# Output projection of a fused attention and gated feed-forward kernel: 32-row heads against dense rows of O

## The chip, the cores and the metric

The kernel runs on one core of a Trainium2 chip. A core has five engines with an instruction queue each: PE (TensorE, the matmul array, whose weight loads are listed as PEld), DVE (VectorE), ACT (ScalarE), POOL (GpSimd) and SP (SyncE, which here only issues transfers). They share the on-chip memory SBUF; PE writes its results into PSUM, eight banks of 128 partitions by 2 KB. Engines wait for one another through semaphores, and each carries out its queue in order. The metric is the device time of one execution in microseconds (us), as the median of several.

## The reference

```python
def _A_ref(x, wqkv, wo):                       # B, S, D = 1, 2048, 640
    H = 32; Dh = D // H                        # 32 heads of 20
    qkv = (x @ wqkv).reshape(B, S, 3, H, Dh).transpose(2, 0, 3, 1, 4)
    q, k, v = qkv[0], qkv[1], qkv[2]
    scores = jnp.einsum("bhqd,bhkd->bhqk", q, k) * Dh ** -0.5
    o = jnp.einsum("bhqk,bhkd->bhqd", softmax(scores), v)
    return o.transpose(0, 2, 1, 3).reshape(B, S, D) @ wo

def _B_ref(x, w1, b1, w2):                     # F = 1536
    h = x @ w1 + b1
    return (h * jnp.tanh(softplus(h))) @ w2

g = sigmoid((x * gate_w).sum(-1, keepdims=True))
return g * _A_ref(...) + (1 - g) * _B_ref(...)
```

Everything is bfloat16. The softmax of 32 heads over 2048 by 2048 scores is 134 million exponentials, which is most of the kernel.

## The kernel before

**Tiling.** Heads go in 8 groups `g` of four, queries in 4 chunks `c` of 512, keys in 16 tiles of 128. A unit is one head by one key tile by one chunk: a score matmul of 32 rows by 128 keys by 512 queries into one PSUM bank, its exponential, and a matmul with V (PV) of 21 columns, whose first column of ones gives the softmax's sum. There are 2048 units. Four heads lie on 32 partitions each, so score matmuls of different heads run side by side, and so do the four PV matmuls of a key tile, which accumulate in bank 6 (`ACC`).

**Two ways to an exponential.** A step (`emit_s`, `emit_e`) computes the scores of two or three units and exponentiates them with one ACT instruction over two or three banks (L1295, "128x1024" or "128x1536") into the ring `ETS`. Beside it DVE takes whole tiles of four units (`x_block`, `emit_x`): it turns each score bank into a 16-bit integer that is the bit pattern of an approximate exponential (L1353), makes two more copies with another offset (L1383), and PE multiplies all three with V, twice with V scaled by POOL (L1409). A tile on DVE so costs four L1353, two L1383, two L1409 and three sets of PV matmuls in place of one. Its bank is one of 7, 5 and 2 (`FLEX`), which `x_block` takes only if DVE or ACT has read it by the time that PE gets there. `third` decides by the same rule whether a step takes three banks.

**Between the steps** PE does tasks: the projections of q, k and v, the feed-forward's two products (`h_task`, `b_task`) and the output projection. They are cut into single accumulation steps, which fill what a step leaves of PE's time.

**After a group** (`group_done`): DVE copies ACC to `OUNG` (L1610), a transfer reads the sums into `RR` (L1613), DVE inverts them (L1617), two transfers spread them over partitions through DRAM (L1618, L1620, into `BCT`), and POOL multiplies (`times`, L1575). The result goes into `QT[:, g, chunk c]`, where the group's queries were: four heads, each on 32 partitions of which 21 carry something. For the program, SP's queue holds these transfers, the feed-forward's weights (L947), the moves of q and k through DRAM and the stores, all in one order.

**Output projection.** `p_task` makes one tile of 128 tokens by 320 columns: eight accumulation steps, one for each group, each with the 128 partitions of `QT` as weights in four quarters of 32 tokens (`quarters`, L526) and the 320 columns of a padded `wo` (`WOG`) streaming by. 24 such tiles belong to chunks 0 to 2. The last chunk's eight tiles are done in two parts, six groups ahead (`part_task`) and two at the very end (`p_task` with `rest`, or `late_mm`), as the last group's softmax ends only then. `load_wo` brings the padded weights and zeros between them.

**Order.** All of it is laid out ahead of time by a planner in the kernel's own Python (`Plan.add`): each operation has an estimated cost, each engine an estimated clock, and rules with some thirty constants decide what comes next. `STRETCHES` gives some of these constants other values from a step on. So any edit moves instructions everywhere.

Of the kernel before, what the change touches and what calls it, by code (L numbers as in the profile page):

```python
# [85 lines left out]
CROWD = 1.357  # L86
# [59 lines left out]

STRETCHES = {
    13: {"CALLED": 3.681, "CROWD": 1.516, "KEPT": 14, "LATER": 0.181, "NEED": 4, "OVER": 0.547, "ROOM": 1.615, "STREAM": 0.46},
    32: {"CALLED": 3.681, "CROWD": 0.992, "FMIN": 0.345, "KEPT": 8, "LATER": 0.181, "LOAD": 0.613, "NEED": 4, "OVER": 0.547, "PATIENCE": 2.71, "ROOM": 1.318, "SLACK": 0.305, "SPUN": 0.635, "STREAM": 0.413, "THIRD": 0.599, "XSLACK": 0.603},
    52: {"CALM": 5, "EAGER": 131, "LATER": 0.553, "OVER": 0.328, "VMIN": 1.54},  # L150
    74: {"BEHIND": 25.336, "CALM": 10, "FREE": 0.172, "MARGIN": -0.397, "ROOM": 1.73, "STREAM": 0.359, "THIRD": 0.926},
    96: {"BEHIND": 25.336, "CALM": 10, "EAGER": 156, "FMIN": 0.177, "FREE": 0.172, "LATER": 0.693, "MARGIN": -0.397, "ROOM": 1.73, "STREAM": 0.359, "THIRD": 0.926},
    118: {"AHEAD": 23, "BEHIND": 23.531, "BUSY": 0.465, "LOAD": 0.723, "NEED": 2, "PATIENCE": 11.956, "SPUN": 0.486, "THIRD": 1.082, "XSLACK": 0.459},
    140: {},
    159: {"BUSY": 0.52, "LATER": 0.268, "PATIENCE": 6.491, "SPUN": 0.578, "STREAM": 0.36},
    177: {"BUSY": 0.716, "FMIN": 0.404, "LATER": 0.268, "PATIENCE": 6.491, "SPUN": 0.578, "STREAM": 0.36},
    197: {"MARGIN": 0.991, "ROOM": 1.736, "XSLACK": 0.222},
    216: {"BEHIND": 24.715, "CALLED": 0.877, "LATER": 0.69, "MARGIN": 0.991, "ROOM": 1.736, "SLACK": 0.232, "SPUN": 0.618, "XSLACK": 0.222},
    236: {"AHEAD": 29, "BEHIND": 24.715, "BUSY": 1.142, "CALLED": 1.095, "KEPT": 12, "LATER": 0.493, "MARGIN": 0.991, "PATIENCE": 9.167, "ROOM": 1.736, "SLACK": 0.232, "SPUN": 0.643, "STREAM": 0.441, "VMIN": 0.744, "XSLACK": 0.222},
    257: {"AHEAD": 45, "BEHIND": 18.952, "BUSY": 1.117, "CALLED": 1.095, "FMIN": 0.076, "FREE": 0.133, "KEPT": 12, "LATER": 0.493, "MARGIN": 0.991, "OVER": 0.11, "PATIENCE": 9.167, "ROOM": 1.736, "SLACK": 0.321, "SPARED": 1, "SPUN": 0.643, "STREAM": 0.441, "VMIN": 0.744, "XSLACK": 0.222},  # L160
    276: {"BUSY": 0.321, "CALM": 4, "CROWD": 1.465, "EAGER": 157, "LOAD": 0.543, "MARGIN": 0.584, "NEED": 4, "PATIENCE": 11.808, "SLACK": 0.257, "SPARED": 1},
    298: {"FREE": 0.157, "LOAD": 0.615, "NEED": 4, "OVER": 0.168, "STREAM": 0.569, "VMIN": 1.094, "XLATE": 11.627},
    319: {"CROWD": 0.991, "FMIN": 0.126, "FREE": 0.036, "MARGIN": 1.148, "SPUN": 0.7},
    341: {"AHEAD": 44, "CROWD": 0.991, "EAGER": 115, "FMIN": 0.126, "FREE": 0.036, "MARGIN": -0.419, "SPUN": 0.668, "THIRD": 0.337},
    360: {"AHEAD": 44, "CROWD": 0.991, "EAGER": 115, "FMIN": 0.126, "FREE": 0.036, "MARGIN": -0.419, "NEED": 4, "SPUN": 0.668, "THIRD": 0.337, "XSLACK": 0.204},
    379: {"AHEAD": 44, "CALM": 5, "CROWD": 1.926, "EAGER": 90, "FMIN": 0.191, "FREE": 0.036, "MARGIN": -0.5, "NEED": 4, "PATIENCE": 12.367, "ROOM": 3.226, "SPARED": 1, "SPUN": 0.668, "THIRD": 0.447, "VMIN": 0.861, "XSLACK": 0.258},
    396: {"CROWD": 1.489, "SLACK": 0.54, "THIRD": 0.417, "XSLACK": 0.47},
    416: {"CROWD": 0.97, "EAGER": 44, "KEPT": 15, "LATER": 0.299, "OVER": 0.128, "STREAM": 0.521},
    438: {"CROWD": 0.97, "EAGER": 44, "FREE": 0.231, "KEPT": 15, "LATER": 0.299, "MARGIN": 0.28, "OVER": 0.128, "PATIENCE": 12.737, "STREAM": 0.521, "THIRD": 0.979, "VMIN": 0.916, "XLATE": 6.721},
    460: {"CROWD": 0.97, "EAGER": 44, "FREE": 0.231, "KEPT": 15, "LATER": 0.299, "MARGIN": 0.28, "OVER": 0.128, "PATIENCE": 12.737, "STREAM": 0.521, "THIRD": 0.979, "VMIN": 0.916, "XLATE": 6.721},  # L170
    481: {"CROWD": 0.97, "EAGER": 44, "FREE": 0.118, "KEPT": 15, "LATER": 0.299, "MARGIN": 0.28, "OVER": 0.06, "PATIENCE": 12.737, "SLACK": 0.161, "STREAM": 0.521, "THIRD": 1.171, "VMIN": 0.916, "XLATE": 6.721},
    501: {"CALLED": 0.845, "CALM": 4, "FMIN": 0.095, "LATER": 0.538, "ROOM": 3.669},
# [129 lines left out]
def bass_gated_mix__softmax_full_mha__dense_activation_mish__prompt_kernel(  # L302
# [123 lines left out]
    def attention(pl, fast):  # L426
# [1140 lines left out]
        def group_done(c, g, step, last):  # L1567
# [39 lines left out]
            while oung_free[m] == "busy":  # L1607
                (norm or lasting).popleft()[1]()
# [459 lines left out]
```

## Time and profile before

| what | value |
|---|---|
| median of 3 runs | 751.69 us (751.41 to 752.72) |
| the profiled execution | 750.51 us, of which the span from first to last instruction is 748.7 us |
| POOL busy | 358.0 us (48%), 695 instructions |
| PEld busy | 276.0 us (37%) |
| DMA | 50.49 MB, 67 GB/s on average, HBM read 39.01 MB and written 8.90 MB |
| granted PE clock | 0.998 of full speed |

The page's busy times are unions of intervals: an instruction counts from its start to its end, also where the next one has begun already. An engine that is 97% busy may thus still be slower than it could be. The idle time of an engine and what ended it stand beside each group of instructions.

### The profile page before, as it was taken

The page shows a single profiled execution, that of the slowest core. Times are in us where ns is not written, and L with a number is a line of the kernel's source. Part 1 is how long each engine was busy: PE and PEld are TensorE (multiplying, and loading weights), DVE is VectorE, ACT ScalarE, POOL GpSimd, SP SyncE. Part 2 cuts the span into 40 slices and gives each one's busy share as a digit, 9 for nine tenths or more (in the row PEclk, how much of TensorE's full clock was granted, in tenths as well). Part 3 has the DMA queues.
Part 4 walks back from the last instruction along what each step waited for, and adds up shares of the span by engine and source line. Part 5 has one row for each costly group of instructions (what it writes and reads, how often), then busy time and mean ns, then how long its engine had stood idle before and what let it go on. Part 6 is the DMA issues. An engine that isn't in the chain of part 4 may idle for free.

```text
span 748.7 us, 26101 instructions
## 1 busy us (share of the span) xinstructions
PE 724.3 (97%) x11336; PEld 276.0 (37%) x11336; DVE 681.1 (91%) x1173; ACT 730.1 (98%) x755; POOL 358.0 (48%) x695
## 2 busy tenths in 40 slices
PE   8999999999999999999999999999999999999996
PEld 3333334334433332233333433334343343333343
DVE  3799999889898989989999999999999999999985
ACT  6999999999999999999999999999999999999995
POOL 3304332115563547322458675163568758575331
PEclk9999999999999999999999999999999999999999
DMA  9312323123133422632132210112221221101001
GB/s 193 104 30 68 96 66 90 35 83 95 37 92 89 127 70 72 183 80 49 46 104 63 58 36 21 52 39 59 62 76 49 67 63 49 56 18 35 17 25 44
DMA packets 78020, 50.49 MB, mean 67 GB/s; under 512 B 21408, under 2 KB 73880, under 8 KB 77848
## 3 DMA queue, kind: packets, MB, share of 16 engines
q1 hardware_dynamic: 75528, 48.24, 23.4%
q8 instruction: 92, 1.51, 0.9%
q10 hardware_dynamic: 2256, 0.47, 0.3%
q14 instruction: 32, 0.26, 0.1%
q0 software_dynamic: 112, 0.01, 0.1%
HBM read 39.01 MB, written 8.90 MB: 64 GB/s over the span
## 4 chain that ended last, share of the span: by engine, by line
ACT 43%; PE 38%; DVE 14%; POOL 3%; issue 1%; DMA 0%; ACTq 0%; POOLq 0%
ACT ETS L1295 42%; PE PS L1268 13%; PE PS L1513 11%; PE PS L526 11%; DVE LN L1353 4%; DVE LN L1383 2%; POOL HB L1049 2%; DVE U L1048 1%; POOL U L1047 1%; DVE U L1052 1%; PE PS L847 1%; DVE HB L1009 1%; ACT W2R L1033 1%; DVE REG L1383 1%; DVE REG L1353 1%
## 5 line engine op out<-in xcount | busy, mean ns | idle before, releaser
L1295 ACT ACTIVATE ETS<-PS 128x1024 bf16<-128x1024 f32 (+1 forms) x724 | 708.5, 1134 | 5.3 <-PE PS L1268 3.6
L1268 PE MATMUL PS<-QT,KT 32*128 32x512 bf16 (+1 forms) x2130 | 285.9, 377 | 10.8 <-ACT ETS L1295 8.3
L1353 DVE TENSOR_SCALAR LN<-PS 128x512 int16<-128x512 f32 x412 | 274.7, 680 | 20.5 <-PE PS L1268 18.7
L1409 POOL TENSOR_SCALAR VS<-V_all 128x84 bf16<-128x84 bf16 x268 | 146.2, 546 | 93.5 <-PE PS L1513 51.3
L1268 PEld LDWEIGHTS PS<-QT,KT 32*128 32x128 bf16 x2130 | 72.3, 91 | 230.9 <-ACT ETS L1295 192.2
L1513 PE MATMUL PS<-ETS,V_all 128*21 128x512 bf16 (+1 forms) x1584 | 148.6, 375 | 0.2 <-ACT ETS L1295 0.2
L1383 DVE TENSOR_SCALAR LN<-LN 128x2048 int16<-128x2048 int16 x186 | 132.7, 717 | 5.6 <-PE PS L1513 4.9
L1049 POOL TENSOR_TENSOR HB<-U,HB 128x128 bf16<-128x128 f16 x192 | 93.1, 517 | 83.8 <-DVE U L1048 83.8
L1575 POOL TENSOR_TENSOR QT<-OUNG,BCT 128x128 bf16<-128x128 f32 x124 | 64.0, 546 | 119.2 <-DMA BCT<-SUMS 119.2
L526 PE MATMUL PS<-XB,REG 128*32 128x256 bf16 (+1 forms) x1800 | 88.0, 295 | 2.5 <-DVE LN L1353 1.0
L1513 PE MATMUL PS<-LN,VS 128*21 128x512 f16 (+1 forms) x844 | 79.0, 377 | 1.2 <-POOL VS L1409 1.0
L526 PE MATMUL PS<-W2R,HB 128*32 128x320 bf16 x1536 | 75.8, 301 | 0.6 <-issue 0.3
L1513 PEld LDWEIGHTS PS<-ETS,V_all 128*21 128x21 bf16 x1584 | 38.2, 90 | 54.5 <-issue 46.5
L1047 POOL TENSOR_SCALAR U<-REG 128x256 f16<-128x256 f32 x72 | 37.3, 541 | 36.3 <-ACT REG L1033 35.1
L526 PEld LDWEIGHTS PS<-XB,REG 128*32 128x32 bf16 x1800 | 42.2, 95 | 28.3 <-issue 19.1
L526 PE MATMUL PS<-WOQ,QT 128*32 128x320 bf16 x1024 | 50.7, 301 | 0.5 <-DVE QT L1601 0.3
L526 PEld LDWEIGHTS PS<-W2R,HB 128*32 128x32 bf16 x1536 | 35.1, 96 | 25.4 <-issue 13.7
L1513 PE MATMUL PS<-LN,V_all 128*21 128x512 f16 (+1 forms) x424 | 40.3, 376 | 0.0
L1353 DVE TENSOR_SCALAR REG<-PS 128x512 int16<-128x512 f32 x56 | 37.4, 679 | 2.9 <-PE PS L1268 2.8
L526 PE MATMUL PS<-XB,WOQ 128*32 128x512 bf16 (+2 forms) x440 | 35.6, 381 | 0.1
L1513 PEld LDWEIGHTS PS<-LN,VS 128*21 128x21 bf16 x844 | 19.9, 89 | 39.0 <-issue 17.9
L1048 DVE TENSOR_TENSOR U<-U 128x1024 f16<-128x1024 f16 x48 | 32.7, 681 | 0.2
(116 smaller groups left out, 531.9 us busy)
## 6 DMA issues: line engine op xcount, KB each, us to landing
REG<-in_B_w_dram SPq DMA_DIRECT2D x36, 320.0 KB, 3.3
BCT<-SUMS SPq DMA_DIRECT2D x31, 256.0 KB
W2R<-in_B_w_dram SPq DMA_DIRECT2D x12, 320.0 KB, 4.5
QT<-QS SPq DMA_DIRECT2D x28, 128.0 KB, 3.0
KT<-KS SPq DMA_DIRECT2D x28, 128.0 KB
KS<-LN SPq DMA_DIRECT2D x16, 128.0 KB, 4.3
QS<-WOQ SPq DMA_DIRECT2D x16, 120.0 KB
W2R<-in_B_w_dram SPq DMA_DIRECT2D x12, 160.0 KB, 4.3
```

What stands on the lines that cost most here:

```text
L526: last = e.matmul(to[at + j:at + j + n, :], w[:, j:j + n], x, start=start, stop=stop, tile_position=(0, at + j))
L847: return lambda e, bank: e.matmul(PS[:, bank, t * n:(t + 1) * n], xt(c)[:, f, t * P:(t + 1) * P], WV[:, f, g * HD:g * HD + n], start=(f == ...
L1047: lift = lambda e, at: e.tensor_scalar(A[:, at], U[:, at], LIFT, LIFT, ALU.mult, ALU.add)
L1048: times = lambda e, at: e.tensor_tensor(A[:, at], A[:, at], B[:, at], ALU.mult)
L1049: last = lambda e, at: e.tensor_tensor(h[:, at], A[:, at], h[:, at], ALU.mult)
L1268: op = pl.add("pe", lambda e, to=to, g=real(g), tile=tile, j=j, cols=cols, c=c, of_q=of_q: e.matmul(to[:, cols], KT[32 * j:32 * j + 32, g, ...
L1295: e_op[s] = pl.add("act", lambda e: e.activation(RING[:, p:p + n, :], scores(s)[:, 0:n, :], AF.Exp, scale=SCALE), [s_op[s], *(pv_slot[b] f ...
L1353: bank_free[bank] = x_ops[bank] = tile["op"] = dve(lambda e: e.tensor_scalar(dst, PS[:, bank, :], SCALE * ULPS, BASE, ALU.mult, ALU.add), ...
L1383: op = pl.add("dve", lambda e: e.tensor_scalar(to, src, SHADES[n] - SHADES[held], None, ALU.add), [made, *deps], cost=SHADE, lock=SHADE - ...
L1409: ops = [pl.add("pool", lambda e, i=i, n=n, src=src: e.tensor_scalar(VS[:, n, i, :, :], src, WEIGHTS[i + 1], None, ALU.mult), [v_done[(rea ...
L1513: lasts[n] = pl.add("pe", lambda e, v=v, j=j, src=src[:, cols], of_q=of_q, begin=begin, end=end: e.matmul(PS[32 * j:32 * j + EW, ACC, of_q ...
L1575: oung_free[m] = bc_read[0] = otn_done[(c, g)] = pl.add("pool", lambda e, some=some: e.tensor_tensor(otn(c, g)[:, some], src[:, some], BC[ ...
```

## The change

**Dense rows.** In the taken program, `times` is followed by transfers for 30 of the 31 groups that it serves (all but group 6 of the last chunk): `ship` writes the group's 128 by 512 to a DRAM scratch `OT`, `land` reads rows 1 to 16 of each of its four heads back to 64 dense partitions, two groups to one block of 128, and once for each chunk a further transfer brings the four rows that are left of all heads (17 to 20) as a fifth block. `ship` goes into the queue two steps after `times` (`SHIP`), `land` four steps after `ship` (`LAND`). `p_task` then has five accumulation steps instead of eight, `part_task` four instead of six; the last two groups of the last chunk stay as they were. `wo` is loaded in the new order of rows, with the padded form for the last two groups only.

**Banks.** `x_block` may take a bank that comes free up to `EARLY` later than PE gets there (0.35 us, in some stretches 0.17 to 0.55), and `third` one up to `SOON` later (0, in some stretches up to 0.28).

**Planning.** Two assumed lock times between DVE and POOL are changed, and all stretches have new constants, with new step numbers.

```diff
+EARLY = 0.35
+SOON = 0.0
+SHIP = 2
+LAND = 4
 STRETCHES = {
-    140: {},
+    141: {"BEHIND": 24.559, "CALLED": 1.144, "EARLY": 0.264, "KEPT": 12, "OVER": 0.186, "SPUN": 0.579},
...
+    OT = nc.dram_tensor("OT", [NC, H, 32, CW], BF16, kind="Internal")
...
+                wo_h = A_wo.rearrange("(h r) c -> h r c", r=DH)
+                pieces = [(f"wm{k}", WQ[:, k, :], wo_h[8 * k:8 * k + 8, 0:16, :], 0.9) for k in range(NFT - 1)]
+                pieces.append(("wr", WQ[:, NFT - 1, :], wo_h[:, 16:DH, :], 0.9))
+                pieces += [(f"wo{j}", WOP[32 * j + 1:32 * j + 1 + DH, :, :], wo_v[j, :, NG - 2:, :], 0.5) for j in range(HG)]
...
         def p_mm(c, t, half, g, groups):
+
+            if fast and g < NFT:
+                rows = P if c < NC - 1 or g < NFT - 1 else 16 * (NG - 2)
+                o, w = otn(c, g)[0:rows, t * P:(t + 1) * P], WQ[0:rows, g, half * HALF:(half + 1) * HALF]
+            else:
+                o, w = otn(c, g)[:, t * P:(t + 1) * P], (WOP[:, g - NG + 2, :] if fast else WOG[:, g, :])[:, half * HALF:(half + 1) * HALF]
...
+        if fast:
+            every = tuple(range(NFT))
+            early, late = (0, 1, 2, 4), (NG - 2, NG - 1)
...
-            if not x and late < THIRD or free is not None and free.t1 + HOP > begin:
+            if not x and late < THIRD or free is not None and free.t1 + HOP > begin + SOON:
...
-                return free is None or free.t1 + HOP <= begin
+                return free is None or free.t1 + HOP <= begin + EARLY
...
+                if fast and (c < NC - 1 or g < NG - 2):
+                    shipping.append((now["step"] + SHIP, lambda: ship(done)))
+                else:
+                    otn_done[(c, g)] = done
+
+            def ship(done):
+                slot = f"os{c % 2}{g % 2}"
+                shipped[(c, g)] = op = shipped[slot] = pl.add("sp", lambda e: e.dma_start(
+                    OT.ap()[c, HG * g:HG * g + HG, :, :].rearrange("j r t -> (j r) t"), otn(c, g)), [done, shipped.get(slot)],
+                    slot, cost=0.45, tail=2.5, bulk=0.3)
+                shipping.append((now["step"] + LAND, lambda: land(op)))
+
+            def land(op):
+                main = 64 * (g % 2)
+                last = g == (NG - 1 if c < NC - 1 else NG - 3)
+                slot = f"ot{c % 2}{g % 2}"
+                landed.setdefault(c, []).append(op)
+                done = otn_done[(c, g)] = landings[slot] = pl.add("sp", lambda e: e.dma_start(
+                    otn(c, g // 2)[main:main + 64, :], OT.ap()[c, HG * g:HG * g + HG, 1:17, :]), [op, landings.get(slot)],
+                    slot, cost=0.45, tail=2.5, bulk=0.2)
+                if last:
+                    rest_done[c] = pl.add("sp", lambda e: e.dma_start(
+                        otn(c, NFT - 1)[0:HD // 5 * (g + 1), :], OT.ap()[c, 0:HG * (g + 1), 17:21, :]), landed[c], f"or{c}",
+                        cost=0.45, tail=2.7, bulk=0.3)
```

Line numbers grow by 6 to 60 through the insertions: L1295 becomes L1321, L1268 L1294, L1513 L1539, L526 L532, L1353 L1379, L1383 L1409, L1613 L1668. Counted over the two programs, in the branch that is taken:

| engine, instruction | before | after |
|---|---|---|
| ACT, exponential of two banks / of three / of one | 642 / 81 / 1 | 700 / 36 / 0 |
| DVE, L1353 (a score bank to integers) | 520 | 540 |
| DVE, L1383 (a shifted copy) | 260 | 270 |
| POOL, L1409 (V scaled) | 268 | 278 |
| PE, quarters of the output projection (L526) | 1024 | 672 |
| PE, PV matmuls | 3192 | 3232 |
| PE, score matmuls | 2130 | 2126 |
| PE, fillers on the keys (L1806) | 8 | 4 |
| SP, transfers | 305 | 374 |

Three places in the two programs' order. The first is ACT, from the point where the kernel reads its safety flag (about a fifth into the program); `ETS` is the ring of exponentials, `W2R<-HB` the feed-forward's tanh. Before:

```order
L1295 ACTIVATE ETS<-PS 128x1024 x7
L1033 ACTIVATE W2R<-HB 128x1024
L1295 ACTIVATE ETS<-PS 128x1024 x2
L1295 ACTIVATE ETS<-PS 128x1536
L1295 ACTIVATE ETS<-PS 128x1024
L1295 ACTIVATE ETS<-PS 128x1536
L1295 ACTIVATE ETS<-PS 128x1024
L1295 ACTIVATE ETS<-PS 128x1536
L1295 ACTIVATE ETS<-PS 128x1024
L1295 ACTIVATE ETS<-PS 128x1536
L1033 ACTIVATE W2R<-HB 128x1024
```

and after:

```order
L1321 ACTIVATE ETS<-PS 128x1024 x3
L1321 ACTIVATE ETS<-PS 128x1536
L1321 ACTIVATE ETS<-PS 128x1024 x7
L1043 ACTIVATE W2R<-HB 128x1024
L1321 ACTIVATE ETS<-PS 128x1024 x11
L1043 ACTIVATE W2R<-HB 128x1024
L1321 ACTIVATE ETS<-PS 128x1024 x29
L1043 ACTIVATE W2R<-HB 128x1024
L1321 ACTIVATE ETS<-PS 128x1024 x32
```

The steps of three banks give way to steps of two, beside each of which DVE takes a bank.

The second is PE at the first tiles of the output projection, a little past the middle of the program; `WOQ,QT` are its quarters, four to an accumulation step. Before:

```order
L526 MATMUL PS<-WOQ,QT 32x320 x12
L1268 MATMUL PS<-QT,KT 128x512 x2
L1513 MATMUL PS<-ETS,V_all 21x512 x4
L526 MATMUL PS<-WOQ,QT 32x320 x8
L1268 MATMUL PS<-QT,KT 128x512 x3
L526 MATMUL PS<-WOQ,QT 32x320 x12
```

and after:

```order
L532 MATMUL PS<-WOQ,QT 32x320 x8
L1294 MATMUL PS<-QT,KT 128x512 x3
L1539 MATMUL PS<-ETS,V_all 21x512 x4
L532 MATMUL PS<-WOQ,QT 32x320 x8
L1294 MATMUL PS<-QT,KT 128x512 x2
L1539 MATMUL PS<-LN,VS 21x512 x4
L532 MATMUL PS<-WOQ,QT 32x320 x8
```

The 32 quarters before are one tile; of the 24 after, 20 are one tile and 4 begin the next.

The third is SP over one group's end, in the part of the feed-forward; `RR<-OUNG`, `SUMS<-RR` and `BCT<-SUMS` are the way of the sums, `REG<-in_B_w_dram` are weights of the feed-forward. Before:

```order
L1613 DMA RR<-OUNG 128x1x16
L947 DMA REG<-in_B_w_dram 128x5x256 x2
L1618 DMA SUMS<-RR 128x16
L1620 DMA BCT<-SUMS 128x1x512
L947 DMA REG<-in_B_w_dram 128x5x256 x2
```

and after:

```order
L1612 DMA OT<-QT 128x512
L1668 DMA RR<-OUNG 128x1x16
L953 DMA REG<-in_B_w_dram 128x5x256
L1622 DMA QT<-OT 64x1x512
L953 DMA REG<-in_B_w_dram 128x5x256 x2
L1673 DMA SUMS<-RR 128x16
L1675 DMA BCT<-SUMS 128x1x512
```

The group before sends its `ship` ahead of this group's reading of the sums and its `land` between two loads of weights.

More of the change, by code (lines that the diff above doesn't have):

```diff
@@ L85 @@
 BUSY = 0.65
-CROWD = 1.357
+CROWD = 1.15
 MARGIN = 0.813
@@ L1156, in p_task @@
             some = late if rest else every
-            needed = [g for g in some if g < NG - 1]
+            needed = [g for g in (late_groups if rest else every_group) if g < NG - 1]
+            tail = [c] if fast and not rest else []
             needed.append(next((k[1] for k, (at, w) in cut.items() if k[0] == c and at <= t * P < at + w), NG - 1))
@@ L1564, in attention @@
         spread_last = []
+        shipping = deque()
+        shipped, landed, landings, rest_done = {}, {}, {}, {}
         end_done = []
@@ L1852, in attention @@
                 grind()
+                for _ in range(len(shipping)):
+                    if shipping[0][0] <= step or not order and step not in slots:
+                        shipping.popleft()[1]()
+                    else:
+                        shipping.rotate(-1)
             ahead = able = 0.0
```

122 lines of the change are left out of this document (70 added, 52 removed).

## The prediction

> **What bounds the kernel now.** I read the busy shares of the engines first, then the chain of work that ended last, then the busy time by stage.
>
> ```profile
> PE 724.3 (97%) x11336; PEld 276.0 (37%) x11336; DVE 681.1 (91%) x1173; ACT 730.1 (98%) x755; POOL 358.0 (48%) x695
> ...
> ACT 43%; PE 38%; DVE 14%; POOL 3%; issue 1%; DMA 0%; ACTq 0%; POOLq 0%
> ```
>
> ACT and PE are both nearly always busy and share the chain almost evenly; DVE follows, and transfers hold nothing.
>
> ```profile
> core 0: us, PE busy (x) PEld busy (x) DVE busy (x) ACT busy (x) POOL busy (x), PEclk, DMA share, GB/s
> 0.00:8.10 8.10, 6.29 (x74) 3.16 (x74) 3.00 (x8) 2.82 (x5) 3.88 (x11) 1.00 0.90 182
> 8.10:98.30 90.20, 87.99 (x1225) 32.67 (x1222) 75.70 (x131) 88.47 (x91) 23.66 (x46) 1.00 0.36 88
> 98.30:362.00 263.70, 258.99 (x3619) 94.62 (x3622) 242.52 (x420) 263.56 (x270) 106.52 (x210) 1.00 0.30 83
> 362.00:740.00 378.00, 368.55 (x6392) 144.56 (x6384) 356.69 (x610) 374.71 (x389) 223.04 (x428) 1.00 0.17 49
> 740.00:748.70 8.70, 2.52 (x40) 0.98 (x40) 3.21 (x8) 0.53 (x1) 0.86 (x1) 0.85 0.26 74
> ```
>
> From the first exponential at 8.1 us to the last at 740 us ACT is idle for 5.2 us in all (731.9 less 88.47, 263.56 and 374.71). So ACT sets the pace, and PE has about 16 us of visible room (731.9 less 715.5) in which it must keep up. What shortens ACT's own list shortens the kernel, as far as PE and DVE follow.
>
> **ACT: the first term.** The instructions overlap at their ends, so the price of one is the distance between starts, not its recorded length.
>
> ```profile
> 723.39 2.47 ACT L1295 ACTIVATE ETS<-PS 128x1024 bf16<-128x1024 f32 x2
> 725.63 1.58 ACT L1295 ACTIVATE ETS<-PS 128x1536 bf16<-128x1536 f32 x1
> 726.96 13.02 ACT L1295 ACTIVATE ETS<-PS 128x1024 bf16<-128x1024 f32 x13
> ...
> L1295 ACT ACTIVATE ETS<-PS 128x1024 bf16<-128x1024 f32 x642 | 612.6, 1085 | 4.7 <-PE PS L1268 3.0 <-PE PS L1513 0.2
> L1295 ACT ACTIVATE ETS<-PS 128x1536 bf16<-128x1536 f32 x81 | 123.5, 1531 | 0.5 <-PE PS L1268 0.5
> ```
>
> These are three rows of ACT's timeline and two of the groups by shape. The exponential of three banks that starts at 725.63 gives way at 726.96: 1.33 us. The two merged in the first row, one of two banks and one of three, take 725.63 - 723.39 = 2.24, which leaves 0.91 for two banks. Both agree with the recorded means: 1531 - 1085 = 0.45 us for one more bank, 0.42 by the starts.
>
> The program now has 58 more of two banks, 45 fewer of three and one fewer of one bank (0.74 us recorded, at most 0.6 by the same overlap): 58 x 0.91 - 45 x 1.33 - 0.6 = 52.8 - 59.9 - 0.6 = **-7.7 us** on ACT. Twenty units have left it for DVE; that they leave is what the room on PE pays for. The tanh instructions and the start are the same.
>
> **PE: does it follow?** Four prices, from rows of PE's timeline:
>
> ```profile
> 330.22 0.61 PE L1513 MATMUL PS<-ETS,V_all 128*21 128x512 bf16 x8
> ...
> 332.72 0.39 PE L1268 MATMUL PS<-QT,KT 32*128 32x512 bf16 x3
> 333.04 0.40 PE L1513 MATMUL PS<-LN,V_all 128*21 128x512 f16 x4
> 333.27 0.39 PE L1513 MATMUL PS<-ETS,V_all 128*21 128x512 bf16 x4
> 333.59 0.39 PE L1268 MATMUL PS<-QT,KT 32*128 32x512 bf16 x3
> ...
> 732.77 1.14 PE L526 MATMUL PS<-WOQ,QT 128*32 128x320 bf16 x28
> 735.47 0.58 PE L526 MATMUL PS<-WOQ,QT 128*32 128x320 bf16 x12
> ```
>
> Four quarters run side by side as one accumulation step; 28 in 1.14 and 12 in 0.58 make 0.56 / 4 = 0.14 us a step. The change takes out 352 / 4 = 88 of them: -12.3 us. A set of four PV matmuls costs 0.61 - 0.40 = 0.21; five more tiles on DVE mean 40 more PV matmuls, 10 sets: +2.1. Four fillers fewer, at the same 0.21: -0.8. ACT has 736 steps in place of 724, and each makes PE switch to scores and back: from 332.72 to 333.04 and from 333.27 to 333.59 are 0.64 us with one PV set in it, so 0.42 without. Twelve more: +5.0. The sum is **-6.0 us**.
>
> So ACT's list shrinks by 7.7 and PE's by 6.0, in a kernel where both are on the chain. Where ACT paces, the gain is 7.7, where PE does, 6.0; I take **-7**, nearer to neither. The 88 steps are saved only from about 400 us on, while three of the five added DVE tiles lie before that. There PE has only what the new stage constants give it, which is why I don't take the whole 7.7.
>
> **DVE.** It gets 20 more conversions and 10 more copies.
>
> ```profile
> 331.68 1.28 DVE L1353 TENSOR_SCALAR LN<-PS 128x512 int16<-128x512 f32 x2
> 332.87 0.68 DVE L1383 TENSOR_SCALAR LN<-LN 128x2048 int16<-128x2048 int16 x1
> 333.47 0.68 DVE L1353 TENSOR_SCALAR LN<-PS 128x512 int16<-128x512 f32 x1
> ...
> 200.00:240.00 40.00, 39.34 (x591) 13.66 (x594) 35.42 (x60) 40.00 (x41) 16.33 (x32) 1.00 0.28 85
> 560.00:600.00 40.00, 38.83 (x656) 15.06 (x655) 39.56 (x69) 39.56 (x42) 30.31 (x57) 1.00 0.20 58
> ```
>
> Starts lie 0.60 apart for both kinds (332.87 to 333.47; 331.68 to 332.87 for two). So 30 x 0.60 = 18 us more in about 742, where DVE was idle for 67.6 (748.7 - 681.1). On the path that is nothing as long as the additions fall where DVE has room, 4.6 us of 40 around 220 us, and not where it has none, 0.4 of 40 around 580. Counted along PE's order, the second half gets two more tiles and the first three. Two tiles there are 12 instructions, 7.2 us at most if nothing of them hides; I count 0 and keep 3 us for the upper end.
>
> **Waits for banks.** `EARLY` and `SOON` let PE stand before a bank that is still being read, and everything behind in its queue stands too: PV of earlier steps, the next scores, and with them ACT. No row shows what this will cost. The lower bound is a gain, the first rival below, if the freer choice smooths PE's queue. The upper bound is all 540 blocks late by 0.35 us, 189 us. The nearest measured thing is PE's room of 16 us, into which late banks must fit to cost nothing; I take 0, and keep a quarter of that room, 4 us, for the upper end.
>
> **Transfers and SP.** 69 more issues.
>
> ```profile
> QT<-QS SPq DMA_DIRECT2D x28, 128.0 KB, 3.0
> ...
> KS<-LN SPq DMA_DIRECT2D x16, 128.0 KB, 4.3
> ...
> 331.79 0.58 SPq L1613 DMA_DIRECT2D RR<-OUNG  x1
> ...
> 341.86 0.23 DVE L1617 RECIPROCAL RR<-RR 128x16 f32<-128x16 f32 x1
> ...
> 719.96 0.56 SPq L1613 DMA_DIRECT2D RR<-OUNG  x1
> ...
> 724.34 0.24 DVE L1617 RECIPROCAL RR<-RR 128x16 f32<-128x16 f32 x1
> ...
> SPq L1620 <- DMA SUMS<-RR: 60.8, 31, 6.8
> ```
>
> The bytes (30 x 128 KB out, 30 x 64 KB back and some, 6.2 MB to 50.5) move beside engines that use a fifth to a third of their time, as the DMA column of the stages shows: nothing. A write like `ship` lands after 4.3 us and a read like `land` after 3.0, so a group's rows are dense some 10 us later; the first projections read groups that ended far earlier. The order counts: SP stands still while `ship` waits for POOL and `land` for `ship`. Behind them stands the reading of the next group's sums. Between that issue and DVE's inversion are 10.1 us at 331.79, 4.4 in the last 75 us: cover for a hold of some microseconds. The last row, of SP's own waits (us in total, times, longest), shows that SP waits through a landing for each group already, about 2 us a time. I take 0.
>
> **The end.** Behind the last exponential both programs run the same chain (last PV, inversion on DVE, 32 quarters, four mixes, stores), 8.7 us; one mix more falls into a pause of DVE there. 0.
>
> **The sum** against the profiled execution: span 748.7 - 7.0 = 741.7, and with the 1.8 us around the span (750.51 - 748.7) 743.5. The median of the runs is 1.2 us above that execution, so 744.7.
>
> **The rivals.**
>
> *PE's stalls shrink as well.* By the stages ACT is idle for 5.2 us, and further time hides in overlapping ends: 642 x 0.91 + 81 x 1.33 + 0.6 = 692.5, and 24 tanh at about 1 us, leave some 15 us of 731.9. If the relieved PE and the wider choice of banks win a third of it, -5 more: 739.7. For it: 38% of the chain lies on PE. Against: twelve more steps. 12%.
>
> *PE or DVE becomes the bound.* The extra blocks meet a full DVE (3 us) or banks that are late (up to 4 us): half or all of the gain goes, 748 to 751.5. For it: DVE at 39.56 of 40. Against: ACT's shorter list is certain from the counts. 15% for 747 to 750.2, and 8% for no difference.
>
> *SP holds up the sums (slower).* If POOL multiplies late, `ship` and `land` are reached one after the other, and SP stands through the whole landing, 4.3 us, before it reads the next group's sums or loads the next weights. DVE then stands at the inversion in its own order, with blocks in banks that PE wants. It decides where SP is held for longer than the cover: 4.4 us less the landing itself in the last three groups, about 8 elsewhere. At 0.5 us for each of 31 groups it is 15 us: 744.7 + 15.5 = 760; if half hides, 752.5. For it: SP already spends 60.8 us of 31 groups standing behind one landing. Against: the steps between `ship` and `land` are about as long as the landing (four at 0.91 to 1.0 us). 10%.
>
> The Trainium skill, "DMA: Bandwidth & Descriptors", section "Anatomy of one DMA — SWDGE (gpsimd) path", says that DMA engines never wait on semaphores, and that any such wait is done by the issuing sequencer before dispatch. By that rule this rival would be the likely case, if the holds were long. The trace agrees that SP is where such waits are spent, with the 60.8 us above, but shows no reader that came too late.
>
> *The change doesn't do what it says*: excluded, as the counts show 672 quarters.
>
> **Numbers.** 742 to 747 has 55%, the larger gain 12%, the smaller one 15%, no difference 8%, slower 10%. A measurement here can tell about 0.2% (1.5 us) from no change. Faster 0.82, same 0.08, slower 0.10. The range 739.5 to 750.5 holds the first three.
>
> **What would show it.** ACT's groups should have 700 and 36 instructions and be idle for no more than about 7 us between first and last; the quarters of the output projection should fall from 50.7 to some 33 us busy; DVE should come to about 700; the inversions (L1672) should have no idle time before them that ends with a transfer. I am wrong if ACT's idle time or the distances between its starts grow by more than 5 us, if PE's waits for DVE before scores grow, or if the rows of DVE name `RR`.

## The result and the profile after

The changed kernel takes **744.26 us** (median of 4 runs, 743.15 to 744.74) against 751.55 us for the kernel before in the same session (4 runs, 750.54 to 752.72): a ratio of 0.990, 95% interval 0.9882 to 0.9919. The forecast was 744.7. The profiled execution took 744.41 us, its span is 742.5 us.

The page of the changed kernel, busy shares and then the chain that ended last:

```profile
PE 721.6 (97%) x11013; PEld 272.2 (37%) x11016; DVE 692.5 (93%) x1203; ACT 722.5 (97%) x767; POOL 366.6 (49%) x705
...
PE 45%; ACT 34%; DVE 15%; POOL 3%; DMA 1%; issue 1%; POOLq 0%
```

ACT's busy time fell by 7.6 us (730.1 before), about as much as the whole kernel. PE's fell by only 2.7, although 352 quarters are gone. The chain now goes over PE more than over ACT (before: ACT 43%, PE 38%).

The groups of the changed kernel by shape (busy time and mean ns, then idle time before them and what ended it):

```profile
L1321 ACT ACTIVATE ETS<-PS 128x1024 bf16<-128x1024 f32 x700 | 657.8, 1077 | 4.7 <-PE PS L1294 3.1 <-PE PS L1539 0.6
L1321 ACT ACTIVATE ETS<-PS 128x1536 bf16<-128x1536 f32 x36 | 54.6, 1521 | 0.3 <-PE PS L1294 0.3
...
L1379 DVE TENSOR_SCALAR LN<-PS 128x512 int16<-128x512 f32 x412 | 273.1, 681 | 11.2 <-PE PS L1294 10.4
...
L1672 DVE RECIPROCAL RR<-RR 128x16 f32<-128x16 f32 x31 | 7.5, 241 | 0.0
```

The exponentials are 700 and 36, and ACT waits no more than before: 5.0 us beside 5.2. DVE's greatest pause, before the conversions into `LN`, shrank from 20.5 us to 11.2. The row of before:

```profile
L1353 DVE TENSOR_SCALAR LN<-PS 128x512 int16<-128x512 f32 x412 | 274.7, 680 | 20.5 <-PE PS L1268 18.7
```

The inversions have no idle time before them: no sum came too late.

The stages of the changed kernel, cut at the same places as before (us, busy time and count of each engine, granted clock, DMA):

```profile
core 0: us, PE busy (x) PEld busy (x) DVE busy (x) ACT busy (x) POOL busy (x), PEclk, DMA share, GB/s
8.10:98.30 90.20, 87.09 (x1183) 33.45 (x1183) 75.55 (x129) 88.43 (x94) 23.82 (x46) 1.00 0.37 88
98.30:362.00 263.70, 260.24 (x3423) 90.81 (x3419) 255.59 (x445) 262.69 (x280) 116.18 (x224) 1.00 0.31 88
362.00:734.00 372.00, 365.93 (x6328) 144.15 (x6332) 355.10 (x615) 368.83 (x391) 221.82 (x424) 1.00 0.22 63
734.00:742.50 8.50, 2.06 (x45) 0.78 (x34) 3.77 (x9) 0.53 (x1) 0.86 (x1) 0.90 0.31 88
```

Between 8.1 and 734 us ACT is idle for 725.9 - 88.43 - 262.69 - 368.83 = 5.95 us, and part of that lies ahead of its first exponential. DVE's additional work sits in the second stage: 255.59 us where it had 242.52. All 20 added conversions start ahead of 362 us (272 of all conversions do, where before it was 252).

**Where the 7 us are.** From the start of the first exponential (8.17 us before, 9.88 after) to the end of the last (739.98 and 733.58, from the trace's records) are 731.8 us before and 723.7 after: **8.1 us less**. The end behind it is 9.0 us beside 8.7. I also summed, over all exponentials but the last, by how much the next start on ACT comes later than 0.905 us (two banks) or 1.331 (three); below these are "stalls". They are 19.7 us before and 19.6 after. So between its first and last exponential ACT's list became shorter, and nothing else happened to ACT.

The profiled execution gave 1.7 us back at the start. First the kernel before, then the changed one, on PE's timeline (start, length, and how many are merged in the row):

```profile
5.77 0.82 PE L614 MATMUL PS<-XB,WOQ 128*20 128x256 bf16 x20 [0.18 <-DVE XB L784]
6.42 0.72 PE L614 MATMUL PS<-XB,REG 128*20 128x256 bf16 x20
```

```profile
5.80 1.25 PE L620 MATMUL PS<-XB,WOQ 128*20 128x256 bf16 x20
6.83 1.28 PE L620 MATMUL PS<-XB,REG 128*20 128x256 bf16 x20
```

The same twenty matmuls start at the same time and take one and a half times as long, the next twenty still longer. That this belongs to the execution and not to the kernel is shown at the end.

**Where PE's relief went.** The windows of the quarters' line (L526 before, L532 after; us, busy, count) up to 362 us and from there, before and then after:

```profile
0.00:362.00 362.00, 102.40 (x1672) 1.00 0.33 87
362.00:748.70 386.70, 162.22 (x3616) 1.00 0.17 49
```

```profile
0.00:362.00 362.00, 86.18 (x1340) 1.00 0.34 90
362.00:742.50 380.50, 161.84 (x3588) 1.00 0.22 63
```

The output projection lies wholly behind 362 us (its first quarter starts at 421 us before, at 425 after). Yet 332 quarters are missing *ahead* of 362 us and only 20 behind (the second row before counts 8 that cross the cut a second time). The groups of the first 362 us say which: before,

```profile
L526 PE MATMUL PS<-W2R,HB 128*32 128x320 bf16 x312 | 15.9, 301 | 0.3 <-issue 0.3
...
L526 PE MATMUL PS<-XB,REG 128*32 128x256 bf16 x80 | 3.8, 273 | 0.0
```

and after:

```profile
L532 PE MATMUL PS<-W2R,HB 128*32 128x320 bf16 x60 | 2.9, 300 | 0.0
```

The new plan does 252 + 80 quarters of the feed-forward later, in the room that the projection left, and so carries the relief into the first half. PE's busy time from 98.3 to 362 us did not fall with it (258.99 to 260.24 us); the added DVE tiles lie there too, with three sets of PV matmuls each in place of one.

### The profile page after: what moved, and what is told of

Read it like the earlier page. It is cut to its first block, busy times and chain, and to the rows that moved or that the text cites. A ratio compares the mean times of both kernels' runs of the same rounds, so it can differ in the third digit from the quotient of the medians.

```text
span 742.5 us, 25540 instructions
## 1 busy us (share of the span) xinstructions
PE 721.6 (97%) x11013; PEld 272.2 (37%) x11016; DVE 692.5 (93%) x1203; ACT 722.5 (97%) x767; POOL 366.6 (49%) x705
## 4 chain that ended last, share of the span: by engine, by line
PE 45%; ACT 34%; DVE 15%; POOL 3%; DMA 1%; issue 1%; POOLq 0%
ACT ETS L1321 33%; PE PS L1294 16%; PE PS L1539 13%; PE PS L532 13%; DVE LN L1379 5%; DVE LN L1409 3%; PE PS L880 2%; POOL HB L1059 2%; DVE REG L1379 1%; DVE U L1058 1%; DVE HB L1019 1%; PE PS L620 1%; POOL U L1057 1%; DMA W2R<-in_B_w_dram 1%; DVE U L1062 1%
## 5 line engine op out<-in xcount | busy, mean ns | idle before, releaser
L1321 ACT ACTIVATE ETS<-PS 128x1024 bf16<-128x1024 f32 (+1 forms) x736 | 700.3, 1099 | 5.1 <-PE PS L1294 3.4
L1294 PE MATMUL PS<-QT,KT 32*128 32x512 bf16 (+1 forms) x2126 | 294.9, 377 | 9.9 <-ACT ETS L1321 6.4
L1379 DVE TENSOR_SCALAR LN<-PS 128x512 int16<-128x512 f32 x412 | 273.1, 681 | 11.2 <-PE PS L1294 10.4
L1435 POOL TENSOR_SCALAR VS<-V_all 128x84 bf16<-128x84 bf16 x278 | 156.0, 561 | 94.9 <-PE PS L1539 60.0
L1294 PEld LDWEIGHTS PS<-QT,KT 32*128 32x128 bf16 x2126 | 75.4, 91 | 233.6 <-ACT ETS L1321 180.5
L1539 PE MATMUL PS<-ETS,V_all 128*21 128x512 bf16 (+1 forms) x1564 | 145.5, 375 | 0.0
L1409 DVE TENSOR_SCALAR LN<-LN 128x2048 int16<-128x2048 int16 x192 | 138.8, 727 | 4.5 <-PE PS L1539 4.3
L1059 POOL TENSOR_TENSOR HB<-U,HB 128x128 bf16<-128x128 f16 x192 | 97.0, 539 | 86.1 <-DVE U L1058 86.1
L1603 POOL TENSOR_TENSOR QT<-OUNG,BCT 128x128 bf16<-128x128 f32 x124 | 60.8, 521 | 110.0 <-DMA BCT<-SUMS 110.0
L532 PE MATMUL PS<-XB,REG 128*32 128x256 bf16 (+1 forms) x1800 | 87.8, 296 | 0.5 <-DVE LN L1379 0.3
L1539 PE MATMUL PS<-LN,VS 128*21 128x512 f16 (+1 forms) x884 | 83.1, 378 | 0.2 <-DVE LN L1409 0.2
L532 PE MATMUL PS<-W2R,HB 128*32 128x320 bf16 x1536 | 76.0, 301 | 0.6 <-DVE LN L1379 0.4
L1539 PEld LDWEIGHTS PS<-ETS,V_all 128*21 128x21 bf16 x1564 | 37.8, 90 | 49.6 <-issue 40.7
L532 PEld LDWEIGHTS PS<-XB,REG 128*32 128x32 bf16 x1800 | 41.1, 95 | 28.6 <-issue 19.4
L532 PEld LDWEIGHTS PS<-W2R,HB 128*32 128x32 bf16 x1536 | 35.5, 96 | 25.9 <-issue 13.1
L1379 DVE TENSOR_SCALAR REG<-PS 128x512 int16<-128x512 f32 x60 | 40.1, 680 | 1.5 <-PE PS L1294 1.5
L1539 PE MATMUL PS<-LN,V_all 128*21 128x512 f16 (+1 forms) x424 | 40.2, 375 | 0.0
L532 PE MATMUL PS<-XB,WOQ 128*32 128x512 bf16 (+2 forms) x440 | 35.6, 382 | 0.2
L1539 PEld LDWEIGHTS PS<-LN,VS 128*21 128x21 bf16 x884 | 20.7, 89 | 41.0 <-issue 25.3
L532 PE MATMUL PS<-WOQ,QT 128*32 128x320 bf16 (+1 forms) x672 | 33.7, 301 | 1.2 <-DVE REG L1379 0.5
L1019 DVE TENSOR_TENSOR HB<-PS,B1F 128x512 bf16<-128x512 f32 x48 | 32.6, 680 | 1.0 <-PE PS L532 1.0
```

Source lines behind the costliest of these rows:

```text
L532: last = e.matmul(to[at + j:at + j + n, :], w[:, j:j + n], x, start=start, stop=stop, tile_position=(0, at + j))
L1019: ev = dve(lambda e: e.tensor_tensor(hb, PS[:, bank, :].rearrange("p (i t) -> p i t", i=2), bias, ALU.add), [last, *b1f, *guarded, *b_read ...
L1059: last = lambda e, at: e.tensor_tensor(h[:, at], A[:, at], h[:, at], ALU.mult)
L1294: op = pl.add("pe", lambda e, to=to, g=real(g), tile=tile, j=j, cols=cols, c=c, of_q=of_q: e.matmul(to[:, cols], KT[32 * j:32 * j + 32, g, ...
L1321: e_op[s] = pl.add("act", lambda e: e.activation(RING[:, p:p + n, :], scores(s)[:, 0:n, :], AF.Exp, scale=SCALE), [s_op[s], *(pv_slot[b] f ...
L1379: bank_free[bank] = x_ops[bank] = tile["op"] = dve(lambda e: e.tensor_scalar(dst, PS[:, bank, :], SCALE * ULPS, BASE, ALU.mult, ALU.add), ...
```

## The experiments

Twelve kernels ran. The first five keep the changed kernel's order and add a cost, so the chip answers how much of it shows. The next three plan anew without one part of the change. The last four keep the order of the kernel before. "Extra" is the difference of a kernel's ratio from 0.990, times 751 us; the interval of 0.990 alone makes it uncertain by 1.4 us. Line numbers shift by a few through the edits, and `...` stands for further lines of code.

### The 88 steps back on PE (e1)

```diff
+            back = {5: 3, 4: 2}.get(len(groups), 0) if fast and g == groups[0] else 0
+            def mm(e, bank):
+                for _ in range(back):
+                    quarters(e, PS[:, bank, 0:HALF], o, w, start=True, stop=True)
...
```

> The changed kernel in its own order, with the 88 accumulation steps put back on PE: each output tile begins with two or three steps whose result is overwritten (352 more quarters, 88 x 0.14 = 12.3 us of PE). The outputs stay the same. My theory (ACT's shorter list is the gain, and PE's relief is what lets ACT keep to it): part of the 12.3 us shows, since PE has about 6 us of visible room between 362 us and the last exponential; 5 to 9 us more than the changed kernel, 749 to 753. Rival 1 (PE is the bound and the gain is PE's): nearly all of it, 755 to 757. Rival 2 (the new plan alone is the gain and the dense rows are not needed): 0 to 2 us, 744 to 746.

Measured: 755.3 us, ratio 1.0058 (1.004 to 1.0076), extra 11.9 of 12.3 us (the two profiled executions differ by 10.8). This is the figure of rival 1, whose other half, that the gain is PE's, e6 tests. From first to last exponential there are 10.1 us more, all of it behind about 410 us, where the steps are. The page's chain, and the row of the exponentials:

```profile
PE 50%; ACT 31%; DVE 13%; POOL 3%; DMA 2%; issue 1%; SPq 0%; POOLq 0%
...
L1326 ACT ACTIVATE ETS<-PS 128x1024 bf16<-128x1024 f32 (+1 forms) x736 | 703.0, 1092 | 12.5 <-PE PS L1299 10.5
```

Of ACT's 12.5 us of waiting 10.5 end with a score matmul: PE has hardly any room in this order, though it is idle for 3%.

### More on PE early (e5)

```diff
+                        for _ in range(2 * (f == 0)):
+                            quarters(e, PS[:, bank, :], WK[:, f, base:base + P], xt(c)[:, f, :], start=True, stop=True)
...
```

and the same with `WQ` in the projection of q.

> The changed kernel in its own order, with 72 accumulation steps of 512 columns added on PE ahead of the k and q projections of the first 320 us or so (36 tasks, two each, overwritten; 72 x 0.21 = 15 us of PE). The outputs stay the same. Where the extra exponentials of the second experiment showed nearly whole, up to about 320 us, ACT seemed to pace. Theory (ACT paces early, PE late): 3 to 8 us of the 15, 747 to 752. Rival (PE paces everywhere): 12 to 15 us, 756 to 759.

Measured: 757.18 us, ratio 1.0072 (1.0049 to 1.0096), extra 12.9 of 15 us, nearly all ahead of 370 us. The rival again: in the first half, too, PE's time shows nearly whole.

```profile
PE 64%; DVE 15%; ACT 15%; POOL 3%; DMA 1%; issue 1%; POOLq 0%
```

### More on ACT (e2)

```diff
...
+                if fast and s % 8 == 5:
+                    e.activation(JUNK[:, 0:1, :], scores(s)[:, 0:1, 0:P], AF.Exp, scale=SCALE)
...
```

> The changed kernel in its own order, with 92 extra exponentials of 128 columns on ACT, one at every eighth step, into a tile that nothing reads; at 0.05 us for one and 0.43 us for 512 columns each should take some 0.16 us, 14.5 us in all. My theory (ACT sets the pace): 9 to 14 us more, 753 to 758. Rival (PE sets the pace and ACT only follows): less than half, 746 to 751.

Measured: 751.88 us, ratio 1.0013 (1.0004 to 1.0023), extra 8.5 of 14.5 us: between the two theories. Followed from exponential to exponential, 5.6 of the 6.3 us added up to 322 us show, about half from there to 552, a third behind. But some 1.3 of the 5.6 arise between 12 and 16 us, where the granted clock of this execution was 0.5 for 3.4 us; without them it is two thirds in the first part, not the "nearly whole" on which the expectation of e5 was built.

### More on DVE (e3)

```diff
+            twice = s % 12 == 3
...
+                if twice:
+                    e.tensor_scalar(JUNK[:, :], PS[:, bank, 0:P], SCALE * ULPS, BASE, ALU.mult, ALU.add)
...
```

> The changed kernel in its own order, with 48 extra conversions of 128 columns on DVE, at every twelfth step ahead of a real one, into a tile that nothing reads; some 0.3 us each, 15 us in all, of about the size of the 18 us that the change adds to DVE. My theory (DVE's additions are hidden in its 50 us of idle time): 0 to 4 us more, 744 to 748. Rival (DVE has become the bound): 8 to 15 us more, 752 to 759.

Measured: 748.33 us, ratio 0.9965 (0.9948 to 0.9981), extra 4.9 of 9.7 us. The time lies just above the theory's range and far below the rival's: half of the work added to DVE isn't hidden where the plan has made no place for it.

### Every ship twice (e4)

```diff
+                more = again[(c, g)] = pl.add("sp", lambda e: e.dma_start(
+                    OT2.ap()[c, HG * g:HG * g + HG, :, :].rearrange("j r t -> (j r) t"), otn(c, g)), [done, again.get(slot)], slot + "x")
...
```

> The changed kernel in its own order, with each of the 30 transfers to DRAM made twice (the second to another scratch, and the transfer back waits for both): 30 more issues of about 0.5 us, 3.8 MB more, and a longer stand of SP before each transfer back. My theory (SP's holds are covered): within 1.5 us of the changed kernel, 743 to 746. Rival (SP's queue holds up the sums or the weights): 3 us or more on top, 747 or later, and DVE idle before the inversion L1672 or its like.

Measured: 745.18 us, ratio 0.9925 (0.9908 to 0.9943), an interval that overlaps the changed kernel's; from first to last exponential 723.9 us beside 723.7. The transfer added to each group is covered.

### Planned anew without the rule for late banks (r1)

```diff
-                return free is None or free.t1 + HOP <= begin + EARLY
+                return free is None or free.t1 + HOP <= begin
```

and `SOON` is taken out of `third` in the same way.

> The changed kernel planned anew with only the rule of the later banks taken back. By its order 592 and 128 exponentials of two and three banks (708.9 us on ACT, 24 more than the changed kernel) and 120 tiles on DVE in place of 135; on PE 30 PV sets and 16 steps fewer and 30 fillers more. Theory (both ACT and PE bind, so a longer list on ACT shows whatever PE saves): 757 to 768. Rival (PE alone is the bound): 738 to 746.

Measured: 767.06 us, ratio 1.0201 (1.0177 to 1.0225). Without the rule DVE gets 120 tiles in place of 135, and ACT has 592 exponentials of two banks and 128 of three: by starts 592 x 0.905 + 128 x 1.331 = 706.1 us, where the changed kernel has 700 x 0.905 + 36 x 1.331 = 681.4. ACT's list is 24.7 us longer and the kernel 23.3 us slower than 0.990 of the before of that session (751.32), while PE falls to 93% busy. The two come close partly by chance, as in the profiled execution the stalls are 3.5 us shorter than the changed kernel's and the end 1.6 longer:

```profile
PE 714.6 (93%) x10971; PEld 271.8 (36%) x10982; DVE 648.7 (85%) x1113; ACT 744.3 (97%) x751; POOL 332.1 (43%) x675
...
ACT 64%; PE 22%; DVE 9%; DMA 4%; issue 1%; POOL 0%; SPq 0%
```

Here nearly two thirds of the chain lie on ACT, with PE relieved of the same 88 steps.

### Planned anew with padded rows (r2)

The output projection, its weights and its order of rows are again those of before, in some ten places; the main one:

```diff
-                if fast and (c < NC - 1 or g < NG - 2):
+                if False:
                     shipping.append((now["step"] + SHIP, lambda: ship(done)))
```

> The changed kernel planned anew without the dense rows: padded groups and no transfers for O as before, with the later banks, the lock times and the new constants. By its order 715 and 30 exponentials of two and three banks (690.6 us on ACT, 1.9 less than before), 132 tiles on DVE, 1024 quarters. Theory (without PE's relief the new constants bring nothing): 752 to 758. Rival (the new constants and later banks are the gain): 744 to 748.

Measured: 766.68 us, ratio 1.0206 (1.0181 to 1.023), worse than expected. ACT's list is shorter than before's (715 x 0.905 + 30 x 1.331 = 687.0 us beside 642 x 0.905 + 81 x 1.331 + 0.6 = 689.4), yet stalls are 30.2 us beside 19.7, and the end behind the last exponential grew from 9 to 15 us. In ACT's timeline:

```profile
744.18 3.81 ACT L1311 ACTIVATE ETS<-PS 128x1024 bf16<-128x1024 f32 x4
757.63 0.53 ACT L1983 ACTIVATE LN<-PS,GATE 128x320 f32<-128x320 f32 x1 [9.64 <-PE PS L532]
```

PE still has projection left when the exponentials are done. The short list without the relief gains nothing in this plan.

### Planned anew with dense rows alone (r3)

```diff
-EARLY = 0.35
+EARLY = 0.0
```

and with it `SOON` and the assumed locks as before, and all stretches with before's constants.

> Dense rows with the transfers, planned anew with the constants of before and no late banks: 597 exponentials of two banks and 122 of three (ACT's list by the starts 597 x 0.905 + 122 x 1.331 = 702.7, 11.2 us longer than before's 691.5), 122 tiles on DVE, 672 quarters on PE. If ACT's list decides, 755 to 764, slower than before in spite of PE's relief; if PE's relief alone made the gain, 740 to 748.

Measured: 770.39 us, ratio 1.0254 (1.0223 to 1.0284): beyond the range on the side of ACT's list, so that PE's relief makes no gain in this plan. Of the 19 us against before the list accounts for 13.3 (702.7 beside 689.4 at the same prices, where the expectation had 691.5), and some 6 more are stalls (25.4 us). In this execution the granted clock was 0.5 from 316.3 to 323.1 and from 592.8 to 599.6 us, and 6.8 us of the stalls lie from 310 to 332 and from 590 to 605; all four executions were granted 0.988 to 0.992 on average. Whether the clock made these stalls or the waits brought the clock down isn't shown. All three of these kernels run on constants that were chosen for another program, and their losses contain that too. They show that no part gains when it is planned so, not what a part is worth by itself.

### Before's order without the 88 steps (e6)

```diff
+            if fast and g in {8: (1, 2, 3), 6: (1, 2)}.get(len(groups), ()):
+                return lambda e, bank: None
```

> The kernel before in its own order, with three of the eight groups left out of each output tile of chunks 0 to 2 and two of the six of each early part of the last chunk, so that this part of the output projection is missing: 88 steps or 12.3 us less on PE, nothing planned anew and no transfers. Theory (PE's relief is the source of the gain, but in an order that was laid out for the longer tiles it only goes as far as ACT's unchanged list): 3 to 6 us less than before, 745 to 748. Rival (the relief is the whole gain and needs no new plan): 8 to 12 us less, 739 to 743. Rival (the gain is ACT's shorter list): 0 to 2 us less, 749 to 751.

Measured: 750.12 us, ratio 0.9988 (0.9976 to 1.0001). 12.3 us less for PE give about 1 us. This is the figure of the second rival, that the gain is ACT's shorter list, which e7 tests.

```profile
ACT 63%; PE 16%; DVE 15%; POOL 4%; issue 1%; DMA 1%; ACTq 0%; POOLq 0%
```

PE's part of the chain falls from 38% to 16%, and ACT's takes its place.

### Before's order with shorter exponentials (e7)

```diff
+            some = CW - 40 * (n == SLOT and fast)
...
-                RING[:, p:p + n, :], scores(s)[:, 0:n, :], AF.Exp, scale=SCALE),
+                RING[:, p:p + n, 0:some], scores(s)[:, 0:n, 0:some], AF.Exp, scale=SCALE),
```

> The order of before, with nothing replanned; the 81 exponentials of three banks cover 472 of each bank's 512 columns (the other 40 keep what the ring held, so the result is not the reference's). By the starts, 0.42 us for 512 columns, that is 81 x 120 x 0.42 / 512 = 8.0 us less on ACT, as much as the change takes from its list, while PE, DVE and the order are those of before. If ACT's list alone decided the time, the kernel would come to 742 to 745, as fast as the changed one. My theory is that the lists of ACT and PE fit one another nearly without room, so that either alone gives little: 748 to 750.5, with more stalls between ACT's starts and PE's chain share above ACT's.

Measured: 749.36 us, ratio 0.9978 (0.9966 to 0.999), as the theory said. The exponentials of three banks took 1.231 us to the next start, so 81 x 0.1 = 8.1 us were cut, and 1.7 gained; stalls grew from 19.7 to 25.1 us. The chain turned the other way:

```profile
PE 49%; DVE 23%; ACT 22%; POOL 4%; issue 1%; DMA 0%; POOLq 0%
```

### Both at once (e8), and the relief early (e9)

e8 is e7 with the edit of e6. e9 is e7 with PE relieved in the first 330 us instead:

```diff
+                    if f in (1, 2):
+                        return lambda e, bank: None
                     return lambda e, bank: quarters(
                         e, PS[:, bank, :], WK[:, f, base:base + P], xt(c)[:, f, :], start=(f == 0), stop=(f == NFT - 1))
```

and the same in the projection of q.

> The same shortened exponentials (8.0 us less on ACT) and also the 88 accumulation steps of the projection left out (12.3 us less on PE), in the order of before. My theory that both lists must shrink together gives 742 to 745.5, more than the sum of the two alone. The rival, that the order itself (the new plan's places of banks and tiles) carries the gain, gives 747 to 750.

> The shortened exponentials in the order of before, as two runs ago, and PE relieved early instead of late: of the five accumulation steps of each early projection of k and q the second and third are left out (so the result is not the reference's), 72 steps of 512 columns, by the rows 0.21 us each, 15 us less on PE, all in the first 330 us; the output projection keeps its 88 steps. Until 330 us the exponentials are 4.0 us shorter; without relief there the two runs before delivered 0.8 to 1.7 us of that. My theory, that ACT's shorter list shows where PE is relieved at the same place, gives 3 us or more of the 4.0 by that point and 746 to 748 in all. The rival, that old places of banks and tiles hold it back whatever PE has to do, gives at most 1.7 by that point and 748.5 to 750.

Measured: e8 747.47 us, ratio 0.9954 (0.9936 to 0.9971); e9 746.94 us, ratio 0.9944 (0.9926 to 0.9961). For e8 my theory fell: both shorter lists give 3.4 us, about the sum of the two alone (0.9 and 1.7), not 7. The time lies in the range of its rival, that the new plan's order itself carries the gain. For e9 the time came as my theory said. Where the gain arises may tell why. The four kernels run the same steps, so the start of the 321st exponential (329.5 us before) and of the last can be set against the kernel before, each counted from the first exponential:

| order of before, with | gained to 329.5 us | gained behind it |
|---|---|---|
| PE relieved late (e6) | 0.3 | 1.3 |
| ACT shorter, 4.1 us ahead and 4.0 behind (e7) | 1.7 | 1.0 |
| ACT shorter, PE relieved late (e8) | 0.8 | 2.2 |
| ACT shorter, PE relieved early (e9) | 2.6 | 0.8 |

To 329.5 us e7 and e8 run the same instructions, so their 1.7 and 0.8 show how far single executions differ. The pattern stands only little out of that: ACT's shorter list shows most in the half in which PE was relieved, 2.2 of 4.0 late and 2.6 of 4.1 early. It isn't all of it in either, where my expectation for e9 asked for 3. So the place of the relief fits these figures, but no run in the order of before gained more than 4.2 of the change's 7.3 us, and none relieved PE in both halves. What the new order adds by itself stays open.

## Why the prediction was right, and where it wasn't

**ACT's list, -7.7: right.** Both the counts and the prices held (0.905 and 1.331 between starts), and the way from first to last exponential became 8.1 us shorter with unchanged stalls. r1 shows the same the other way round: 24.7 us more on the list, 23.3 us more in time. A shorter list alone doesn't leave the stalls as they are, though: in the order of before 8.1 us less gave 1.7 (e7), and 3.4 with PE relieved as well (e8).

**PE, -6.0: its prices held, its place didn't.** Over the changed kernel's whole trace 4, 8, 12 and 16 quarters of the projection take 0.24, 0.38, 0.52 and 0.66 us from start to start (medians), and scores with one, two and three PV sets behind them at least 0.65, 0.86 and 1.08. That is 0.14 us a step, 0.22 a PV set and 0.43 for the switch, as in the sum. The added steps of e1 and e5, 12.3 and 15 us by the rows, show as 11.9 and 12.9. But "PE has about 16 us of visible room" was a wrong reading. PE's idle time between its waits wasn't room here: work added in this order shows nearly whole, which neither its idle 3% nor its chain share told. The Trainium skill, "Perfetto Trace Analysis", section "Identifying the Most-Contended Engine", calls matmul busy share a poor measure of how close one is to the limit, and points instead to the matmul work done against the peak and to the share of weight loads. Here that second share was 37% in both kernels, and in its order PE could take nearly nothing more; the measurement decides against reading it as headroom in this kernel. The first was not worked out.

**"The 88 steps are saved only from about 400 us on": wrong, and the reason for not taking the whole 7.7 with it.** By the windows, 332 of the 352 quarters are saved ahead of 362 us, since the plan puts the feed-forward off. That only three of the five added tiles lie ahead of it was wrong too: the trace has all 20 conversions there. In the fixed order of before the same relief, late, gave 1 us, and even with a shorter ACT 3.4 (e6, e8); with relief in the other half more of the gain arose there, little above the spread (e9). That the postponing is what makes the early gain fits all of this, but no run of the changed kernel without the postponing was made, so it is argued and not shown.

**The -7 between the two terms: right in size by luck, as two errors offset each other.** ACT's stalls did not grow, so -8.1 arose between the exponentials; 1.7 was lost in the start of the profiled execution, which I had as "the same", and 0.2 at the end. That execution is 6.1 us below its counterpart (750.51 to 744.41), the medians 7.3.

**DVE, 0: right for this plan, wrong as a rule.** Busy time grew by 11.4 us and the pauses before its conversions fell by 9.3; ACT's stalls did not grow by it. But e3 shows that work without a place in the plan costs half of its length. That it was free here fits its place: all of it went ahead of 362 us, where DVE was idle for 21 of 264 us in the second stage, and not behind, where the prediction feared for two tiles.

**Waits for banks, 0: right, but the rule itself was underrated.** The late banks cost ACT no stalls. One sign of being wrong did come in small: PE's and its weight loads' idle time before scores that ended with a conversion grew from 0.4 us (2 times) to 3.0 (9 times), while over all of PE's instructions such idle time is 15.7 us before and 15.6 after. I priced the late banks only as a risk, while they are what gives DVE its tiles: without the rule the planner, with the same constants, finds 120, not 135.

**Transfers and SP, 0: right.** `ship` landed after 2.6 us, where I had 4.3 from the nearest row, and SP's waits, behind `ship`, for POOL and for the landing of the sums, are (total, times, longest):

```profile
OT<-QT SPq DMA_DIRECT2D x30, 128.0 KB, 2.6
...
SPq L1675 <- DMA SUMS<-RR: 52.5, 31, 4.1
...
SPq L1622 <- DMA OT<-QT: 31.4, 17, 4.2
...
SPq L1612 <- POOL QT L1603: 24.0, 6, 12.6
```

SP does stand for 55 us in the new transfers, as the slower rival had it, but nobody was late for it: no inversion waited, and doubling the ships changed nothing that can be told apart (e4).

**Of the rivals** none came. Stalls did not shrink (19.7 to 19.6). PE or DVE did not become the bound, but e1, e5 and e3 show how near that was: 12 us more on PE, and the change would have been a loss of 0.6%.

## What to carry to other kernels

In an order laid out so that every engine just keeps up, taking work from one engine can pay little and adding to it much: here 12.3 us less on PE gave 1 us and 12.3 us more cost 11.9, 8.1 us less on ACT gave 1.7 and 14.5 us more cost 8.5. The counts of the pacing engine in the new program, times the distance between starts, gave the gain here, and the loss in r1. They do so only where the stalls stay as they are, which they did not in e7, e8 and r2, so the count is a forecast under that condition. A plan can move relief to another stage, so count each engine's work by stage in the new order before saying where a saving falls.

## What was not expected of the hardware

The start of the first exponential falls into two groups over the fourteen profiled executions. In eight it lies at 8.0 to 8.3 us of the span, in six at 9.7 to 10.0 (the changed kernel, e1, e4, e7, e9 and r1). The kernel isn't what decides: e6 and e8 start at 8.2, e7 and e9, in the same order, at 9.9 and 9.7. PE's first matmul starts at 1.2 us in all of them. The trace's record of the granted clock begins at 4.1 to 5.7 us in the first group and at 9.2 to 10.5 in the second, and until then the first matmuls run at the slower pace of the rows above (1.25 us for twenty in place of 0.82), though the windows print a clock of 1.00 for that stage. The Trainium skill, "TensorE: Matmul & The Clock Gate", section "What's actually happening", has the clock come up after about 3.4 us of work, at a point that depends on a free-running window; these executions agree that it varies by execution, and their spread, 4.1 to 10.5 us, is wider than the plus or minus half a microsecond that the page gives. So 1.7 us, a quarter of this change's gain, can hang on one profiled execution's start: compare from the first exponential on, and trust medians for the rest.
